# VectorE adds exponential tiles before the softmax row sum in six more units of a fused attention and MLP kernel

## The chip, the cores and the metric

The kernel runs on one core of a Trainium2 chip. The metric is the device time of one execution in microseconds (us), the median of several runs. Before the change it is 419.66 us, median of 3 runs (419.33 to 421.46). A core has a matrix engine (TensorE, "PE" in the profile, with its weight loads as "PEld"), VectorE ("DVE"), ScalarE ("ACT"), GpSimd ("POOL"), and DMA queues, most of which are issued by SyncE ("SP"). [...]engines wait for each other with semaphores.

## The reference

Attention with RMS-normalised queries and keys, for 8 batches of 12 heads, sequence 448, head size 64, followed by a two-layer MLP with a leaky ReLU. Everything in and out is float32.

```python
q_n, k_n = rmsnorm(q, g_q), rmsnorm(k, g_k)          # over the head size, 64
scores = (q_n @ k_n^T) / 8
attn = exp(scores - max(scores))
attn = attn / (sum(attn) + 1e-9)                     # the row sum
x = attn @ v                                         # -> (8*448, 12*64)
h = x @ w_in                                         # 768 -> 2048
out = maximum(0.01 * h, h) @ w_out                   # 2048 -> 768
```

## The kernel before

The heads are taken four at a time: a "unit" `u` is one group of four heads of one batch, so there are 24 units (`NU = 24`, three to a batch). The 448 keys of a unit are cut into seven steps `t` (`NS = 7`). For each step TensorE computes scores into one of two PSUM slots, and ScalarE takes the exponential into `et[:, t]`, a tile of 128 partitions by 2 by 448 in fp16.

A unit has four stages `d`: scores and exponentials of step 0, then 1 and 2, then 3 and 4, then 5 and 6. Between them TensorE is filled with items of the MLP from a queue, for an earlier batch.

```python
STEPS = ((0,), (1, 2), (3, 4), (5, 6))
def fill(u, d, jobs):
    ...                                   # how many items of the queue this stage takes
    while queue and debt[0] >= queue[0][0] * 0.5:
        c, fn = queue.pop(0)
        fn()                              # an MLP item: matmuls on TensorE
        debt[0] -= c
        if jobs:
            jobs.pop(0)()                 # one job behind each item
    flush()                               # work that the last item put off
    for job in jobs:
        job()                             # and the rest of the jobs
```

The row sum is a matmul of ones with the exponential tiles, accumulated in PSUM over the tiles. It happens one unit later, in stage 0 of unit `u + 1`. In most units it is `zcol`: for each tile four matmuls with a 128x32 block of ones and 224 columns, each into its own 32 PSUM partitions. In the first few units and the last it is `zsum_slot`: for each tile four matmuls with a 64x64 block of ones and 448 columns.

```python
def zsum_slot(u):
    ...
    ets = z_tiles(u)
    for i, e in enumerate(ets):
        for r in range(2):
            for a in range(2):
                nc.tensor.matmul(s["zt"][r][64 * a:64 * a + 64, 0:S], ones16[64 * r:64 * r + 64],
                                 e[64 * r:64 * r + 64, a], start=(i == 0), stop=(i == len(ets) - 1))

ADDED = {u: 4 for u in (10, 11, 13, 16, 17, 19)}
ADDED[NU - 1] = 5

def add_e(u):                             # VectorE sums the first ADDED[u] tiles into one
    s = st[u]
    s["ea"] = zpool.tile([P, 2, S], FP16, tag="ea", name="ea")
    for t in range(1, ADDED[u]):
        nc.vector.tensor_tensor(s["ea"], s["et"][:, 0] if t == 1 else s["ea"], s["et"][:, t], op=ALU.add)

def z_tiles(u):                           # what TensorE has left to sum
    s = st[u]
    ets = [s["et"][:, t] for t in range(NS)]
    return ets[ADDED[u]:] + [s["ea"]] if "ea" in s else ets

def zcol(u):
    ...
    ets = z_tiles(u)
    for i, e in enumerate(ets):
        for y in range(2):
            for a in range(2):
                c = 32 * (2 * y + a)
                nc.tensor.matmul(s["zc"][c:c + 32, 0:HS], onesr, e[:, a, HS * y:HS * y + HS],
                                 start=(i == 0), stop=(i == len(ets) - 1))
```

The main loop, cut to the parts that matter here. `shift_max` (VectorE) takes a bound on the scores from step 0 and spreads it on a diagonal `dg`; `shift_mm` (TensorE, then VectorE) turns that into the bias `eb` of the exponentials. Between the two, TensorE does the previous unit's product with v (`pv_slot`, `pv`) and its row sum.

```python
for u in range(3, NU):
    for d in range(4):
        if d > 0 or u > 3:
            qk(u, STEPS[d])                       # scores
            if d == 0:
                shift_max(u)
                ...
                if narrow(u - 1):                 # 4 <= u - 1 < 23
                    pv_slot(u - 1)
                    zcol(u - 1)
                    shift_mm(u)
                    pv_out(u - 1)                 # ScalarE frees the slot of pv
                else:
                    zsum_slot(u - 1)
                    pv(u - 1)
                    shift_mm(u)
                    zinv(u - 1)                   # ScalarE: 1 / row sum
            ex(u)                                 # exponentials
            if d == 0 and narrow(u - 1):
                zcol_ln(u - 1)
        if d == 2 and u in ADDED and u < NU - 1:
            add_e(u)
            xmul_sb(u - 1)                        # VectorE: pv times 1 / row sum
        jobs = []
        ...
        if d == 0:
            ...
            if u < 6:
                prep_sqp(u + 3)                   # GpSimd: squares for the norm
        if d == 1 and narrow(u - 1) and not 5 <= u < 8 and u not in ADDED:
            xmul_pool(u - 1)                      # the same product on GpSimd
        ...
        if d == 1 and 5 <= u < NU - 1:
            job(prep_g, u + 1)
        if u + 2 < NU:
            if d == 1:
                for ti in range(2):
                    job(prep_ssq, u + 2, ALL, (ti,))      # VectorE: sums of squares
            if d == 2:
                job(prep_rinv, u + 2)                     # ScalarE
                for ti in range(2):
                    job(prep_norm, u + 2, ALL, (ti,))     # VectorE
        ...
        if d == 1 and 4 <= u < 8:
            job(weight_sum, u - 4, 0)                     # VectorE
        ...
        fill(u, d, jobs)
```

The second MLP layer is done with fewer block products in some places, for which VectorE forms sums and differences of blocks of its operand (`sa`, by `s1` to `s4`). In units 8, 14 and 20 an MLP item puts off the first two of them (`s1`, `s2`) to the next `flush()`.

Of the kernel before, what the change touches and what calls it, by code (L numbers as in the profile page):

```python
# [18 lines left out]
def kernel(  # L19
# [18 lines left out]
    NU = B * NQ  # L38
# [91 lines left out]
    ALL = (0, NS)  # L130
# [7 lines left out]
    def buf(u, name):  # L138
        if name not in st[u]:
            shape, dtype, bufs = SHAPES[name]  # L140
            st[u][name] = prep_p.tile(shape, dtype, tag=name[:2] if bufs == 3 and name != "qkT" else name, bufs=bufs, name=name)
        return st[u][name]
# [14 lines left out]
    def prep_ssq(u, c=ALL, tis=BOTH):  # L157
        for ti in tis:
            nc.vector.tensor_reduce(buf(u, "ssq")[:, ti, :, c[0]:c[1]], buf(u, f"sq{ti}")[:, :, c[0]:c[1]],  # L159
                                    axis=AXL.X, op=ALU.add)  # L160
# [41 lines left out]
    def qk(u, steps):  # L202
        st[u]["sT"] = []
        for t in steps:
            sT = slot()
            score(u, t, (sT[:, 0], sT[:, 1]))
            st[u]["sT"].append((t, sT))
# [17 lines left out]
    def shift_max(u):  # L225
        s = st[u]
        sT = s["sT"][0][1]
        if isinstance(sT, list):
            pm2 = small.tile([P, 2], FP32, tag="pm2", name="pm2")
            for a in range(2):  # L230
                nc.vector.tensor_reduce(pm2[:, a:a + 1], sT[a][:, 0:S], axis=AXL.X, op=ALU.max)
            s["spare"] = sT[0]
            nc.vector.tensor_reduce(s["spare"][:, 511:512], pm2, axis=AXL.X, op=ALU.max)
        else:
            s["spare"] = sT[:, 0]
            nc.vector.tensor_reduce(s["spare"][:, 511:512], sT[:, :, 0:S], axis=AXL.XY, op=ALU.max)  # L236
        s["dg"] = small.tile([P, P], FP16, tag="dg", name="dg")
        nc.vector.tensor_tensor(s["dg"], ident16, s["spare"][:, 511:512].broadcast_to([P, P]), op=ALU.mult)
# [4 lines left out]
    def shift_mm(u):  # L243
        s = st[u]
        if u > 0 and "pslot" in st[u - 1]:
            pb = st[u - 1]["pslot"][:, :, S:S + 64]
            for x in range(2):
                nc.tensor.matmul(pb[:, x], onesp, s["dg"][:, 64 * x:64 * x + 64], start=True, stop=True)
            nc.vector.tensor_reduce(s["spare"][:, 510:511], pb, axis=AXL.XY, op=ALU.max)  # L249
        else:  # L250
            if "pb" not in s:
                shift_bank(u)
            pb = s["pb"]
            nc.tensor.matmul(pb[:, 0:P], onesp, s["dg"], start=True, stop=True)
            nc.vector.tensor_reduce(s["spare"][:, 510:511], pb[:, 0:P], axis=AXL.X, op=ALU.max)
        s["eb"] = small.tile([P, 1], FP32, tag="eb", name="eb")
        nc.vector.tensor_scalar(s["eb"], s["spare"][:, 510:511], -1.0, DELTA, op0=ALU.mult, op1=ALU.add)

    def gate(u):
        nc.gpsimd.tensor_copy(gate_t, buf(u, "n16")[:, 1, NS - 1, 1, D - 1:D])  # L260
# [21 lines left out]

    HS = S // 2
    ADDED = {u: 4 for u in (10, 11, 13, 16, 17, 19)}
    ADDED[NU - 1] = 5

    def add_e(u):
        s = st[u]
# [3 lines that stand above are left out]
# [6 lines left out]
    def zcol(u):  # L298
        s = st[u]
        s["zc"] = aux([P, 512], FP32, "zc")  # L300
# [8 lines that stand above are left out]
    def pv_slot(u):  # L309
        s = st[u]  # L310
        s["pslot"] = slot()
        s["pv"] = [s["pslot"][:, r] for r in range(2)]
        pv(u)
# [21 lines left out]
    def xmul_sb(u):  # L335
        xmul_pool(u, nc.vector)

    def xmul_pool(u, eng=nc.gpsimd):
        s = st[u]
        b, g = divmod(u, NQ)  # L340
        if b not in xts:
            xts[b] = xpool.tile([P, NQ, 2, S], FP16, tag="xt", name="xt")
        eng.tensor_tensor(xts[b][:, g], s["x32"], s["rz"], op=ALU.mult)  # L343
# [375 lines left out]
    def narrow(u):  # L719
        return 4 <= u < NU - 1  # L720
# [46 lines left out]
    with tc.manual_schedule():  # L767
# [182 lines left out]
# [3 lines that stand above are left out]
                    qk(u, STEPS[d])  # L953
                    if d == 0:
                        shift_max(u)
                        if u == 6:
                            xmul_sb(u - 2)
                        if narrow(u - 1):
# [3 lines that stand above are left out]
                            pv_out(u - 1)  # L962
# [4 lines that stand above are left out]
                            zinv(u - 1)  # L967
                    ex(u)
                    if d == 0 and narrow(u - 1):
                        zcol_ln(u - 1)  # L970
                if d == 2 and u in ADDED and u < NU - 1:
                    add_e(u)
                    xmul_sb(u - 1)
                jobs = []

                def job(fn, *args):
                    jobs.append(lambda: fn(*args))

                if d == 0:
                    if u == 3:  # L980
                        prep_norm(4)
                        gate(4)
                    elif narrow(u - 1):
                        if u < NU - 1:
                            job(zcol_inv, u - 1)
                    else:
                        xmul(u - 1)
                    if u + 4 < NU:
                        job(load, u + 4)
                    if u + 3 < NU:  # L990
                        load_v(u + 3)
                    if u < 6:
                        prep_sqp(u + 3)
                if d == 1 and narrow(u - 1) and not 5 <= u < 8 and u not in ADDED:
                    xmul_pool(u - 1)
                if u == NU - 1:
                    if d == 1:
                        job(zcol_inv, u - 1)
                if fed(u, d) and u > 3:
                    push(u // NQ - 1)  # L1000
                if (u, d) in ((3, 1), (4, 0)):
                    for ti in range(2):
                        prep_tr(u + 1, ti, VV)
                if d == 1 and 5 <= u < NU - 1:
                    job(prep_g, u + 1)
                if u + 2 < NU:
                    if d == 1:
                        for ti in range(2):
                            job(prep_ssq, u + 2, ALL, (ti,))
                    if d == 2:  # L1010
                        job(prep_rinv, u + 2)
                        for ti in range(2):
                            job(prep_norm, u + 2, ALL, (ti,))
                        if u > 3:
                            job(prep_trd, u + 2)
                if d == 1 and 4 <= u < 8:
                    job(weight_sum, u - 4, 0)
                if d == 0 and 5 <= u < 9:
                    job(weight_sum, u - 5, 1)
                if d == 2 and 6 <= u < 8:  # L1020
                    job(xmul_sb, u - 1)
                if u == NU - 2 and d == 0:
                    for n, tile_ in ((1, (raws, "rq", 3)), (2, (raws, "rk", 3)), (3, None), (4, (prep_p, "sq", 3))):
                        job(win_sum, n, 1, tile_)
                    for n in (3, 1, 2, 4):
                        job(x_sum, LATE, n)
                if u == NU - 1 and d == 3:
                    job(add_e, u)
                    job(xmul_sb, u - 1)
                if d == 3 and 6 <= u < NU - 3:  # L1030
                    for ti in range(2):
                        job(prep_sq, u + 3, ALL, (ti,))
                fill(u, d, jobs)
# [39 lines left out]
```

## Time and profile before

| | |
|---|---|
| Median time (lowest to highest of 3) | 419.66 us (419.33 to 421.46) |
| Span of the profiled execution | 418.4 us |
| TensorE busy | 402.0 us, 96% of the span |
| VectorE busy | 290.5 us, 69% |
| ScalarE busy | 303.6 us, 73% |
| GpSimd busy | 68.6 us, 16% |
| Mean TensorE clock granted | 0.99 of full speed |

The profile is of one execution. It has the busy time of each engine, the idle time of an engine before each group of instructions together with what ended it, the chain of work that ended last (followed back from the last instruction, at each step to what released it), and a timeline. In a timeline line stand the start and the length in us, then engine, line of the program, operation, and `output<-inputs` with shapes and the count; a bracket gives the idle time ahead of it and what ended it. "PE L306" are the row sums by `zcol`, "PE L280" those by `zsum_slot`, "DVE L291" the adds of `add_e`, "PE L248" and "PE L254" the matmuls of `shift_mm`, and "DVE L236" and "DVE L238" the two operations of `shift_max`.

### The profile page before, as it was taken

How to read it: one execution, taken by the hardware profiler on the slowest of the kernel's cores; microseconds unless marked ns; L12 is line 12 of the kernel's file. 1: busy time of each engine (PE TensorE's matmuls, PEld its weight loads, DVE VectorE, ACT ScalarE, POOL GpSimd, SP SyncE). 2: the span in 40 equal slices, each digit the busy share in tenths (PEclk: the TensorE clock that was granted, in tenths of full speed). 3: DMA queues.
4: the chain of work that ended last, by engine and by line, in shares of the span. 5: the costliest groups of instructions: out<-in, count | busy, mean ns of one | idle time of the engine just before them, and what ended most of it. 6: DMA issues, size and time to landing. Idle time of an engine off the chain costs nothing.

```text
span 418.4 us, 9417 instructions
## 1 busy us (share of the span) xinstructions
PE 402.0 (96%) x3871; PEld 220.6 (53%) x3871; DVE 290.5 (69%) x469; ACT 303.6 (73%) x474; POOL 68.6 (16%) x70
## 2 busy tenths in 40 slices
PE   7877999999999999999999999999999999999995
PEld 6544444555455444455445554455445557558863
DVE  5788675787658757767648757768548787557762
ACT  5998877868987679867986679967986657653600
POOL 1868422300020100020011100011001101000000
PEclk9699999999999999999999999999999999999999
DMA  6999998889664786677565787568552460032023
GB/s 202 268 254 251 240 250 137 194 161 209 166 154 68 209 193 148 169 162 175 153 144 107 205 171 173 148 130 196 171 111 46 119 152 14 2 83 78 0 56 96
DMA packets 71950, 62.41 MB, mean 149 GB/s; under 512 B 36324, under 2 KB 67044, under 8 KB 71908
## 3 DMA queue, kind: packets, MB, share of 16 engines
q1 hardware_dynamic: 61312, 49.62, 46.4%
q0 software_dynamic: 10272, 11.80, 17.8%
q8 instruction: 30, 0.49, 0.5%
q10 hardware_dynamic: 324, 0.39, 0.3%
q14 instruction: 12, 0.10, 0.1%
HBM read 45.61 MB, written 11.01 MB: 135 GB/s over the span
## 4 chain that ended last, share of the span: by engine, by line
PE 80%; ACT 8%; DVE 8%; issue 2%; DMA 1%; SPq 0%; DVEq 0%; ACTq 0%
PE hps L385 27%; PE sT L199 8%; PE sT L363 5%; PE ma L467 5%; PE md L467 5%; ACT et L218 4%; PE bank L587 4%; PE mc L467 4%; PE bank L467 4%; PE op L426 4%; PE mb L467 3%; PE zc L306 3%; DVE n L171 2%; PE sT L467 2%; PE bank L426 1%
## 5 line engine op out<-in xcount | busy, mean ns | idle before, releaser
L218 ACT ACTIVATE et<-sT,eb 128x896 f16<-128x896 f32 x166 | 159.3, 1009 | 18.8 <-PE sT L199 17.0
L385 PE MATMUL hps<-xt,win 128*128 128x448 f16 x600 | 120.8, 353 | 0.2 <-DVE xt L372 0.2
L385 PEld LDWEIGHTS <-win 128*128 128x128 f16 x612 | 56.8, 98 | 58.2 <-issue 9.7
L379 ACT ACTIVATE gt<-hps 128x448 f16<-128x448 f32 x100 | 53.9, 555 | 6.3 <-PE hps L385 5.4
L199 PE MATMUL sT<-qkT 64*64 64x448 f16 x664 | 53.2, 368 | 3.0 <-ACT et L218 1.9
L159 DVE TENSOR_REDUCE ssq<-sq 128x14 f32<-128x896 f32 (+2 forms) x49 | 50.3, 1058 | 0.7 <-ACT sq L148 0.7
L467 PEld LDWEIGHTS <-sa 128*128 128x128 f16 x352 | 32.8, 98 | 26.3 <-issue 6.1
L128 POOL DMA_DIRECT2D vt<-in_v_dram x24 | 17.9, 746 | 172.1 <-PE sT L363 164.7
L318 ACT COPY x<-sT 128x896 f32<-128x896 f32 x19 | 17.2, 905 | 35.4 <-DVE sT L249 35.4
L171 DVE TENSOR_TENSOR n<-rq,rinv 128x896 f16<-128x896 f32 (+2 forms) x25 | 27.6, 1107 | 13.6 <-ACT rinv L165 10.5
L467 PEld LDWEIGHTS <-gt 128*128 128x128 f16 x264 | 25.2, 98 | 19.7 <-issue 3.2
L199 PEld LDWEIGHTS <-qkT 64*64 64x64 f16 x672 | 15.2, 105 | 36.8 <-issue 33.2
L343 POOL TENSOR_TENSOR xt<-x,rz 128x896 f16<-128x896 f32 x9 | 19.0, 2111 | 81.8 <-DMA rz<-zs 81.8
L363 PE MATMUL sT<-et,vt 64*64 64x448 f16 x532 | 28.5, 349 | 0.3
L426 PE MATMUL op<-wout,gt 128*128 128x384 f16 x160 | 28.4, 326 | 0.0
L236 DVE TENSOR_REDUCE sT<-sT 128x1 f32<-128x896 f32 x22 | 24.1, 1094 | 4.7 <-PE sT L199 4.7
L363 PEld LDWEIGHTS <-vt 64*64 64x64 f16 x672 | 20.7, 107 | 11.3 <-issue 1.7
L171 DVE TENSOR_TENSOR n<-rk,rinv 128x896 f16<-128x896 f32 (+2 forms) x26 | 26.1, 1011 | 0.0
L426 PEld LDWEIGHTS <-gt 128*128 128x128 f16 x192 | 17.6, 98 | 14.3 <-issue 3.0
L467 PE MATMUL ma<-wout,gt 128*128 128x384 f16 x128 | 23.5, 326 | 0.0
L448 DVE TENSOR_TENSOR sa<-gt 128x512 f16<-128x512 f16 (+1 forms) x15 | 8.2, 545 | 16.9 <-ACT gt L379 12.2
L291 DVE TENSOR_TENSOR ea<-ea,et 128x896 f16<-128x896 f16 x15 | 9.4, 625 | 13.6 <-ACT et L218 13.3
(142 smaller groups left out, 541.5 us busy)
## 6 DMA issues: line engine op xcount, KB each, us to landing
rq<-in_q_dram SPq DMA_DIRECT2D x24, 448.0 KB, 3.7
rk<-in_k_dram SPq DMA_DIRECT2D x24, 448.0 KB, 5.3
out_dram<-ost SPq DMA_DIRECT2D x52, 192.0 KB, 3.1
rz<-zs SPq DMA_DIRECT2D x76, 112.0 KB, 2.3
vt<-in_v_dram POOLq DMA_DIRECT2D x24, 224.0 KB, 5.2
win<-in_moe_w_in_dram POOLq DMA_DIRECT2D x8, 384.0 KB, 13.4
wout<-in_moe_w_out_dram POOLq DMA_DIRECT2D x2, 1536.0 KB, 27.9
out_dram<-ost SPq DMA_DIRECT2D x4, 96.0 KB, 2.1
```

The source lines that it names most:

```text
L128: nc.gpsimd.dma_start(vts[u % NV].rearrange("p a t d -> p a (t d)"), rows(v, u))
L159: nc.vector.tensor_reduce(buf(u, "ssq")[:, ti, :, c[0]:c[1]], buf(u, f"sq{ti}")[:, :, c[0]:c[1]], axis=AXL.X, op=ALU.add)
L171: nc.vector.tensor_tensor(buf(u, "n16")[:, ti, c[0]:c[1]].rearrange("p s a d -> p a s d"), src[:, :, c[0]:c[1]], buf(u, "rinv")[:, ti, :, ...
L199: nc.tensor.matmul(banks[a][64 * r:64 * r + 64, 0:S].rearrange("p (t x) -> p t x", t=NS), kT(u, r, a, t), qT(u, r, a), start=True, stop=True)
L218: nc.scalar.activation(s["et"][:, t], sT[:, :, 0:S], AF.Exp, bias=s["eb"], scale=1.0)
L236: nc.vector.tensor_reduce(s["spare"][:, 511:512], sT[:, :, 0:S], axis=AXL.XY, op=ALU.max)
L343: eng.tensor_tensor(xts[b][:, g], s["x32"], s["rz"], op=ALU.mult)
L363: nc.tensor.matmul(s["pv"][r][64 * a:64 * a + 64, 0:S], vts[u % NV][64 * r:64 * r + 64, a, t], s["et"][64 * r:64 * r + 64, t, a], start=(t ...
L379: nc.scalar.activation(dst, src, AF.Prelu, bias=0.0, scale=1.0, alpha=0.01)
L385: nc.tensor.matmul(hps[:, 0:S], win16[:, kt // 2, kt % 2, ts(ft, P)], xt[:, kt // 2, kt % 2], start=(kt == 0), stop=(kt == KT - 1))
L426: nc.tensor.matmul(op2[:, 0:HC], gt[:, ft, ds(col(t), P)], wout16[:, ft, ds(HC * half, HC)], start=(ft == 0), stop=(ft == FT - 1))
L467: nc.tensor.matmul(bank[:, 0:HC], a[:, f], b[:, f], start=(first and f == 0), stop=(f == HF - 1), skip_group_check=not first)
```

## The change

VectorE sums exponential tiles in six more units, so that TensorE has fewer tiles left in the row sum. In units 3 and 4 it sums the first five tiles, at stage 2, ahead of the jobs of that stage. In units 8, 14 and 20 it sums the first three, at stage 1: there the two sums of squares and the adds become one job, which comes ahead of the put-off operand sums `s1` and `s2`. In unit 22 it sums the first three, as the third job of stage 1 (an empty job keeps the place). The conditions around `xmul_sb` and `xmul_pool` are kept such that the product with the inverse row sum stays where it was in all these units.

```diff
     ADDED = {u: 4 for u in (10, 11, 13, 16, 17, 19)}
-    ADDED[NU - 1] = 5
+    ADDED.update({3: 5, 4: 5, NU - 1: 5})
+    ADDED.update({u: 3 for u in (8, 14, 20, 22)})
@@
-                if d == 2 and u in ADDED and u < NU - 1:
+                if d == 2 and ADDED.get(u, 0) > 3 and u < NU - 1:
                     add_e(u)
-                    xmul_sb(u - 1)
+                    if u > 4:
+                        xmul_sb(u - 1)
@@
-                if d == 1 and narrow(u - 1) and not 5 <= u < 8 and u not in ADDED:
+                if d == 1 and narrow(u - 1) and not 5 <= u < 8 and ADDED.get(u, 0) < 4:
                     xmul_pool(u - 1)
@@
                     if d == 1:
-                        for ti in range(2):
-                            job(prep_ssq, u + 2, ALL, (ti,))
+                        if ADDED.get(u) == 3:
+                            job(lambda u: (prep_ssq(u + 2), add_e(u)), u)
+                        else:
+                            for ti in range(2):
+                                job(prep_ssq, u + 2, ALL, (ti,))
@@
                 if d == 2 and 6 <= u < 8:
                     job(xmul_sb, u - 1)
+                if d == 1 and u == NU - 2:
+                    jobs.append(lambda: None)
+                    job(add_e, u)
```

## The prediction, made before the changed kernel ran

> **What bounds the kernel now.** I read the shares of busy time first, then the chain that ended last, then the waits, then the timeline around the places that the change touches. The first two lines below are from the page of the kernel before: busy times, and the chain by engine.
>
> ```profile
> PE 402.0 (96%) x3871; PEld 220.6 (53%) x3871; DVE 290.5 (69%) x469; ACT 303.6 (73%) x474; POOL 68.6 (16%) x70
> ...
> PE 80%; ACT 8%; DVE 8%; issue 2%; DMA 1%; SPq 0%; DVEq 0%; ACTq 0%
> ```
>
> TensorE is busy for 96% and holds 80% of the chain. All the waits of TensorE for another engine add up to about 11 us, and most of them lie before 45 us. So a microsecond of matmuls taken out between 55 and 360 us is a microsecond off the end, provided TensorE does not start to wait for what replaces it. The saving is read from the row sums. The chain in order of time (start, length, what) shows one of each form, with what stands behind it:
>
> ```profile
> 55.89 1.32 PE sT L280 x28
> 57.21 1.32 PE pv L363 x28
> 58.53 0.18 PE pb L254
> ...
> 70.70 1.32 PE sT L363 x28
> 72.02 0.78 PE zc L306 x28
> 72.81 0.17 PE sT L248 x2
> ```
>
> Unit 3's row sum (L280) costs 1.32 us for 7 tiles, or 0.189 per tile. Unit 4's (L306) costs 0.78 for 7 tiles. The matmuls of one tile run side by side in the array: 28 of them, 259 ns each, take 0.78 us. A unit that already has four tiles added gives the marginal cost. Unit 16, in the timeline:
>
> ```profile
> 257.53 0.47 PE L306 MATMUL zc<-et,onesr 128*32 128x224 f16 x12
> 257.54 0.29 DVE L238 TENSOR_TENSOR dg<-ident,sT 128x128 f16<-128x128 f16 x1
> 257.83 0.27 PE L306 MATMUL zc<-ea,onesr 128*32 128x224 f16 x4
> ...
> 258.03 0.23 PE L248 MATMUL sT<-dg,onesp 128*128 128x64 f16 x2
> ```
>
> From 257.53 to the next matmul at 258.03 are 0.50 us for 4 tiles, against 0.79 for 7 in the units without adds (193.30 to 194.09): 0.097 us per tile and a fixed 0.11.
>
> [...]the 22 adds it has took 616 to 627 ns. [...]A `weight_sum` (L442) of 0.95 us took 1.66 where it began at 63.37, while GpSimd's square ran from 62.54 to 64.22: it ended 0.8 us after GpSimd. That bears on unit 3, below.
>
> **The change part by part.** Adding n tiles on VectorE costs n - 1 adds and takes n - 1 tiles from TensorE.
>
> Added on VectorE: 4 adds in each of units 3 and 4, 2 in each of 8, 14, 20, 22, together 16 x 0.625 = 10.0 us. Taken from TensorE: 4 x 0.189 = 0.75 us (unit 3), 4 x 0.097 = 0.39 (unit 4), 4 x 2 x 0.097 = 0.78 (the rest). That is 64 matmuls and 1.92 us at the most. The 10 us count only where they hold something up, so I go through the gaps.
>
> *Unit 3, stage 2.* The timeline around it:
>
> ```profile
> 48.90 2.07 DVE L159 TENSOR_REDUCE ssq<-sq 128x14 f32<-128x896 f32 x2
> 50.05 1.68 POOL L152 TENSOR_TENSOR sq<-rk 128x896 f32<-128x896 f32 x1 [0.71 <-DVE ssq L159]
> 50.87 1.90 ACT L218 ACTIVATE et<-sT,eb 128x896 f16<-128x896 f32 x2
> 53.75 1.09 DVE L171 TENSOR_TENSOR n<-rq,rinv 128x896 f16<-128x896 f32 x1 [2.78 <-issue]
> ```
>
> VectorE is idle for 2.78 us here, and four adds need 2.5. But the first add meets GpSimd's square, [...]so I let it end at about 52.25; the second at 52.9, the third at 53.5 and the fourth at 54.15 (tile 4 is ready at 52.77). The two norms then end near 56.25, and `shift_max` of unit 4, now at 56.01, starts 0.2 to 0.3 us late: `dg` at 57.7 instead of 57.43. With only three tiles in the row sum, TensorE reaches `shift_mm` at 58.47 - 0.75 = 57.72. So the saving here is 0.75, or 0.6 if `dg` comes last. I count 0.65. What follows (1 / row sum on ScalarE, the product on VectorE, the first MLP item that waits for it at 59.88) hangs on these matmuls and moves up with them.
>
> *Unit 4, stage 2.* VectorE is idle from 65.03 to 68.50, waiting for ScalarE's `rinv`. Tiles 3 and 4 are ready at 66.7 and 67.6, so the last add ends near 68.25, ahead of the norm. Nothing is delayed. The row sum of three tiles is 0.40 us from 71.95, to 72.35; `dg` is done at 72.24, and `shift_mm` can follow an end of `dg` after 0.05 us (177.94 to 177.99 in unit 12). So it starts at 72.35 instead of 72.74, and 0.39 is gained.
>
> *Units 8, 14, 20, stage 1.* The timeline of unit 14:
>
> ```profile
> 213.20 1.08 DVE L159 TENSOR_REDUCE ssq<-sq 128x14 f32<-128x896 f32 x1
> 214.81 1.92 ACT L218 ACTIVATE et<-sT,eb 128x896 f16<-128x896 f32 x2
> 217.83 0.43 DVE L448 TENSOR_TENSOR sa<-gt 128x512 f16<-128x512 f16 x1 [3.54 <-ACT gt L379]
> 218.29 0.43 DVE L451 TENSOR_TENSOR sa<-sa,gt 128x512 f16<-128x512 f16 x1
> 218.47 2.19 POOL L343 TENSOR_TENSOR xt<-x,rz 128x896 f16<-128x896 f32 x1 [7.17 <-DMA rz<-zs]
> 218.63 1.08 DVE L159 TENSOR_REDUCE ssq<-sq 128x14 f32<-128x896 f32 x1
> ```
>
> The gap of 3.54 us before `s1` takes the second sum of squares (to 215.3), and the adds end near 216.5 and 217.4, as tiles 1 and 2 come at 215.8 and 216.7. `s1` waits for ScalarE until 217.83 anyway. The 1.08 us that the second reduction took behind `s2` come free; I give nothing for that[...]. Unit 20 has the same gap (4.86 us), unit 8 one of 3.81. The saving is 0.19 each at `shift_mm`: `dg` was done 0.43 us before it in unit 15 (226.86 against 227.29), and in units 9 and 21 the same. Sum 0.58.
>
> *Unit 22.* VectorE waits 1.51 us before 346.89. The adds would end near 346.0 and 346.65 (tile 2 at 345.8), just before the copy needs the engine. In unit 23 `dg` ends at 357.02 and `shift_mm` starts at 357.31, so 0.19 fits.
>
> Sum: 0.65 + 0.39 + 0.58 + 0.19 = 1.8 us. On 419.66 this makes 417.9.
>
> **The rivals.** *VectorE's delay takes the place of the matmuls.* Between `shift_max` and `shift_mm` the row sum is also cover for VectorE: in unit 12, behind a row sum of four tiles, `shift_mm` already waits for `dg`. If the adds of unit 3 or 4 ran later than I think, these two savings (1.1 us) would go and the time would be 419. Against it: both gaps are nearly as long as the adds, and the rest of the units keep five tiles.[...]
>
> *The gain is taken up later.* In unit 9 one matmul (L467 at 144.65) waits 0.55 us for VectorE, which was blocked behind GpSimd's product (a norm of 1.08 us took 2.33). If that product is tied to its DMA and not to TensorE, up to 0.55 us of what units 3, 4 and 8 gained stays there, and the time is 418.4. If the shift parts the two, the wait vanishes and it is 417.4. Elsewhere the chain goes through ScalarE and VectorE only in pieces that begin at a TensorE instruction, so they move along.
>
> *The reordering itself helps.* Sums of squares done 1 us earlier let `rinv` start earlier. ScalarE waited only 0.15 us for them in unit 14, so this is worth at most 0.2 us in three units: 417.3.
>
> *More work makes VectorE the bound.* With 300.5 of 418 us it is still at 72%; against it.
>
> **Range and chances.** The matmuls cap the saving at 1.9 us, or 2.5 with a lost wait. The three runs lie within 0.3 us of each other but for one at 421.46, so I allow 0.4 us for the medians. The absorbing rivals reach 419.2. Range 416.9 to 419.2. Two per cent would be 8.4 us, which no step here comes near in either direction.
>
> **What would show it right or wrong.** In the changed profile: 64 matmuls fewer (about 3807), 16 DVE instructions more (485), DVE about 10 us and PE about 2 us apart from before. L291 should have 38 adds near 625 ns, except the first of unit 3, which should take over 1 us. From the start of L306 to L248 there should be 0.40 us in unit 5 and 0.60 in 9, 15, 21, 23, with no idle line "PE <- DVE dg" over 0.1 us. From the start of L280 to L254 in unit 4 there should be 2.0 us instead of 2.75. A longer span, a norm of unit 5 that ends after 56.5, or new waits for DVE on TensorE would show the first rival.

## The result, and the profile after

The changed kernel takes 418.12 us, median of 6 runs (417.61 to 419.21), against 419.80 for the kernel before (6 runs, 419.33 to 421.46). The ratio is 0.9958, with a 95% interval of 0.9938 to 0.9978: 0.4% faster, inside the predicted range and 0.2 us from the predicted 417.9. A second series gave 418.11 against 419.90 (0.9956, interval 0.9943 to 0.9970).

Two lines of the page of the changed kernel, busy times and the chain by engine:

```profile
PE 398.9 (96%) x3807; PEld 219.2 (53%) x3807; DVE 301.6 (72%) x485; ACT 303.6 (73%) x474; POOL 68.6 (16%) x70
PE 80%; DVE 8%; ACT 8%; issue 2%; DVEq 0%; ACTq 0%
```

64 matmuls are gone and 16 VectorE instructions have come, which add 11 us of VectorE time. TensorE's busy time fell by 3.1 us, more than the 2 us predicted; 2.0 of these lie between the starts of `shift_mm` in units 3 and 23 (311.4 to 309.4 us), where the matmuls were taken out, and the rest before and behind that. TensorE still holds 80% of the chain. By these totals the trade went through as drawn.

Where the time went is best read from one instruction that every unit has, the matmul of `shift_mm` (L254 up to unit 4, L248 from unit 5). Its start in the two traces, with the change from one row to the next as the step:

| start of `shift_mm` in unit | before | after | difference | step |
|---|---|---|---|---|
| 3 | 42.82 | 42.48 | -0.34 | (start of the program) |
| 4 | 58.47 | 57.44 | -1.03 | -0.69 |
| 5 | 72.74 | 71.27 | -1.47 | -0.44 |
| 9 | 131.64 | 129.98 | -1.66 | -0.19 |
| 10 | 148.47 | 146.10 | -2.37 | -0.71 |
| 15 | 227.29 | 224.73 | -2.56 | -0.19 |
| 21 | 322.51 | 320.31 | -2.20 | +0.36 |
| 23 | 357.31 | 354.90 | -2.41 | -0.19 |
| end of span | 418.4 | 416.0 | -2.4 | 0.0 |

In units left out the difference moves by 0.02 us at most. The first row is the prologue, whose end lies between 0.7 us earlier and 1.5 us later than before in the traces below; no part of the change is in it. From there on the steps add up to 2.07 us, while the medians differ by 1.7 to 1.8; the other 0.3 us are not accounted for. Five steps are those of the prediction. Two are not: 0.71 us gained in unit 9, where the change does nothing, and 0.36 lost in unit 20, where 0.19 should have been gained.

Unit 3's adds in the timeline of the changed kernel, and what follows:

```profile
49.70 1.68 POOL L152 TENSOR_TENSOR sq<-rk 128x896 f32<-128x896 f32 x1 [0.71 <-DVE ssq L159]
50.53 1.33 DVE L292 TENSOR_TENSOR ea<-et 128x896 f16<-128x896 f16 x1
51.97 2.08 DVE L292 TENSOR_TENSOR ea<-ea,et 128x896 f16<-128x896 f16 x3
53.97 1.08 DVE L171 TENSOR_TENSOR n<-rq,rinv 128x896 f16<-128x896 f32 x1
...
57.10 0.29 DVE L238 TENSOR_TENSOR dg<-ident,sT 128x128 f16<-128x128 f16 x1
57.44 0.23 PE L254 MATMUL pb<-dg,onesp 128*128 128x128 f16 x1
```

The first add began while GpSimd's square ran, took 1.33 us instead of 0.62, and ended 0.48 us behind the square. All four are done at 54.05, the norm follows without a gap, and `dg` ends 0.05 us before the matmul that reads it: here VectorE comes last, by a hair. In unit 5 the row sum is down to three tiles, and in unit 14 the adds lie in the gap ahead of `s1` (L449):

```profile
70.87 0.38 PE L307 MATMUL zc<-et,onesr 128*32 128x224 f16 x8
71.07 0.27 PE L307 MATMUL zc<-ea,onesr 128*32 128x224 f16 x4
71.27 0.23 PE L248 MATMUL sT<-dg,onesp 128*128 128x64 f16 x2
...
213.51 0.62 DVE L292 TENSOR_TENSOR ea<-et 128x896 f16<-128x896 f16 x1 [2.07 <-ACT et L218]
214.41 0.63 DVE L292 TENSOR_TENSOR ea<-ea,et 128x896 f16<-128x896 f16 x1 [0.27 <-ACT et L218]
215.46 0.43 DVE L449 TENSOR_TENSOR sa<-gt 128x512 f16<-128x512 f16 x1 [0.42 <-ACT gt L380]
```

And this is the step that went the wrong way, around the start of unit 21:

```profile
312.57 2.08 POOL L344 TENSOR_TENSOR xt<-x,rz 128x896 f16<-128x896 f32 x1 [8.61 <-ACT uu L164]
312.63 2.30 DVE L458 TENSOR_TENSOR sa<-gt,sa 128x512 f16<-128x512 f16 x1
...
319.97 0.29 DVE L238 TENSOR_TENSOR dg<-ident,sT 128x128 f16<-128x128 f16 x1
320.31 0.22 PE L248 MATMUL sT<-dg,onesp 128*128 128x64 f16 x2 [0.49 <-DVE dg L238]
```

GpSimd's product (L344) came late, an operand sum of 0.41 us (L458) was caught behind it for 2.30, VectorE never made that up, and nearly eight microseconds later TensorE waited 0.49 us for `dg`.

### The profile page after: what moved, and what is told of

Its sections match the earlier page's. It is cut to its first block, busy times and chain, and to the rows that moved or that the text cites. A ratio compares the mean times of both kernels' runs of the same rounds, so it can differ in the third digit from the quotient of the medians.

```text
span 416.0 us, 9315 instructions
## 1 busy us (share of the span) xinstructions
PE 398.9 (96%) x3807; PEld 219.2 (53%) x3807; DVE 301.6 (72%) x485; ACT 303.6 (73%) x474; POOL 68.6 (16%) x70
## 4 chain that ended last, share of the span: by engine, by line
PE 80%; DVE 8%; ACT 8%; issue 2%; DVEq 0%; ACTq 0%
PE hps L386 27%; PE sT L199 8%; PE sT L364 5%; PE ma L468 5%; PE md L468 5%; ACT et L218 5%; PE mc L468 5%; PE bank L588 4%; PE bank L468 4%; PE op L427 4%; PE mb L468 2%; PE zc L307 2%; DVE n L171 2%; PE warm L766 2%; PE sT L468 2%
## 5 line engine op out<-in xcount | busy, mean ns | idle before, releaser
L171 DVE TENSOR_TENSOR n<-rq,rinv 128x896 f16<-128x896 f32 (+2 forms) x25 | 26.2, 1050 | 9.5 <-ACT rinv L165 9.5
L344 POOL TENSOR_TENSOR xt<-x,rz 128x896 f16<-128x896 f32 x9 | 18.9, 2102 | 79.5 <-DMA rz<-zs 63.6
L292 DVE TENSOR_TENSOR ea<-ea,et 128x896 f16<-128x896 f16 x25 | 15.6, 625 | 15.6 <-ACT et L218 14.7
L292 DVE TENSOR_TENSOR ea<-et 128x896 f16<-128x896 f16 x13 | 8.8, 675 | 11.6 <-ACT et L218 11.6
```

The source lines that it names most:

```text
L171: nc.vector.tensor_tensor(buf(u, "n16")[:, ti, c[0]:c[1]].rearrange("p s a d -> p a s d"), src[:, :, c[0]:c[1]], buf(u, "rinv")[:, ti, :, ...
```

## The experiments

Three theories stood at the start. *The trade*: each step is the matmuls taken out, the adds are free, and the order of jobs is neutral. *The order*: moving the second sum of squares ahead of `s1` is what gains or loses. *Chance*: the steps in units 9 and 20 only show where one DMA landed in that execution. Later a fourth was needed.

**Units 3 and 4 alone.** The adds of the other four units are left out, and with them their order of jobs and the empty job of unit 22.

```diff
     ADDED.update({3: 5, 4: 5, NU - 1: 5})
-    ADDED.update({u: 3 for u in (8, 14, 20, 22)})
```

> The adds in units 3 and 4 alone; the other four units are as before. Theory (TensorE pays for the row sums and VectorE's adds are free): 1.1 us below the kernel before; the matmul behind the bound on the scores (L254, L248) starts 0.7 us earlier in unit 4, another 0.4 in unit 5, and no unit after that gains or loses more, but for a wait of about 0.55 us for VectorE that GpSimd's product can put anywhere. Rival (the order of jobs in units 8, 14, 20 gives the gain): under 0.6 us. First add of unit 3 about 1.3 us[...].

Measured: 418.37 us against 420.14, ratio 0.9958 (0.9942 to 0.9974). Steps of -0.68 and -0.44 in units 4 and 5 as expected. Unit 9 gained 0.71 again, and unit 12 lost 0.42. The medians differ by 1.8 us where 1.1 was expected; the steps of the trace add up to 1.4.

**Units 8, 14, 20 and 22 alone.**

```diff
-    ADDED.update({3: 5, 4: 5, NU - 1: 5})
+    ADDED.update({NU - 1: 5})
     ADDED.update({u: 3 for u in (8, 14, 20, 22)})
```

> The adds in units 8, 14, 20, 22 alone, with their order of jobs; units 3 and 4 are as before. Theory: 0.76 us below the kernel before, in four steps of 0.19 us at the starts of units 9, 15, 21, 23. Rival[...]: unit 21 starts with a wait for dg of 0.5 us again, and the whole is 0 to 0.3 us. Rival (order helps): over 1 us.

Measured: 418.86 us, ratio 0.9978 (0.9966 to 0.9989). The four steps came as 0.19, 0.19, 0.20 and 0.19, that of unit 21 too, without a wait, though the order of jobs there is that of the change. A further 0.35 came in unit 9. By the medians the whole is 1.3 us, where the rival that the order helps had asked for over 1; the next run tests that rival by itself.

**The order alone**, with both new lines of `ADDED` left out.

```diff
-                        if ADDED.get(u) == 3:
-                            job(lambda u: (prep_ssq(u + 2), add_e(u)), u)
+                        if u in (8, 14, 20):
+                            job(lambda u: prep_ssq(u + 2), u)
```

> No new adds at all: only the second sum of squares goes ahead of the operand sums in units 8, 14 and 20. Theory: the same as the kernel before within 0.2 us. Rival (the order costs time[...]): 0.2 to 0.6 us slower, with a wait for dg in unit 21. Rival (order helps, as sums of squares come earlier): 0.2 to 0.6 us faster.

Measured: 419.98 us, ratio 0.9995 (0.9985 to 1.0006). Every step after the prologue is 0.01 or less, but for +0.12 in unit 9. The order alone is worth nothing.

**All adds, and all matmuls.** VectorE does the 16 adds, and TensorE sums all seven tiles all the same.

```diff
-        return ets[ADDED[u]:] + [s["ea"]] if "ea" in s else ets
+        return ets[ADDED[u]:] + [s["ea"]] if "ea" in s and u not in (3, 4, 8, 14, 20, 22) else ets
```

> All adds of the change are done and left unused in units 3, 4, 8, 14, 20, 22: TensorE sums all seven tiles there as before. So VectorE has its 10 us more and TensorE keeps its 64 matmuls. Theory: the same as before within 0.3 us, because every add lies in a gap. Rival (VectorE's work delays the path): 0.5 us or more slower.

Measured: 420.19 us, ratio 1.0005 (0.9994 to 1.0016). All 10 us of adds cost nothing that can be seen; no unit's start moved by over 0.01 us, but for -0.37 in unit 9.

**Fewer matmuls, and no adds.** The tiles that VectorE would have added are left out of the row sum, so the result lacks them.

```diff
     def z_tiles(u):
         s = st[u]
         ets = [s["et"][:, t] for t in range(NS)]
+        if u in NEW:                      # NEW = (3, 4, 8, 14, 20, 22)
+            return ets[ADDED[u] - 1:]
@@
     def add_e(u):
+        if u in NEW:
+            return
```

> The changed kernel with the new adds left out, and the tiles that they would have summed left out of the row sum too (its output has too small a row sum in units 3, 4, 8, 14, 20, 22). TensorE does the same 64 matmuls fewer, VectorE has no extra work. Theory (the matmuls are the whole gain, the adds are free): the same as the changed kernel within 0.3 us, thus about 1.7 us below the kernel before; unit 4's step is 0.75 instead of 0.69, because dg no longer comes late. Rival (the adds cost something that the savings hide): 0.5 us or more below the changed kernel.

Measured: 418.20 us against 419.90, ratio 0.9951 (0.9931 to 0.9970), with a span of 415.9 us against the changed kernel's 416.0. Unit 4's step is 0.76 and unit 5's 0.39, the others are the same, and so are the two odd ones: -0.71 in unit 9 and +0.37 in unit 20, with the same wait of 0.49. Its unit 20 and the start of unit 21, to be held against the last fence of the changed kernel:

```profile
312.76 2.07 POOL L349 TENSOR_TENSOR xt<-x,rz 128x896 f16<-128x896 f32 x1 [8.96 <-DMA rz<-zs]
312.80 2.97 DVE L171 TENSOR_TENSOR n<-rq,rinv 128x896 f16<-128x896 f32 x1
...
320.16 0.22 PE L248 MATMUL sT<-dg,onesp 128*128 128x64 f16 x2 [0.49 <-DVE dg L238]
```

Here the norm is the operation that is caught behind the product (2.97 us instead of 1.09). So the wait comes without the adds as well. This run and the one before it settle the trade: the gain is TensorE's, and the adds cost 0.07 us at the start of unit 4, of which unit 5 gives 0.05 back.

**The second sum of squares put back behind `s2`.**

```diff
-                            job(lambda u: (prep_ssq(u + 2), add_e(u)), u)
+                            job(lambda u: (prep_ssq(u + 2, ALL, (0,)), add_e(u)), u)
+                            job(prep_ssq, u + 2, ALL, (1,))
```

> The changed kernel with the second sum of squares of units 8, 14, 20 put back behind the operand sums, and only the adds ahead of them. [...]no wait for dg at the start of unit 21, whenever the product lands, and steps of 0.19 us in units 9, 15, 21, 23. Time: 0 to 0.3 us below the changed kernel. If the wait in unit 21 only came from a late DMA, the order makes no difference.

Measured: 418.47 us, ratio 0.9966 (0.9954 to 0.9978). A miss: the wait at the start of unit 21 is not gone but longer, 0.86 us, and the step +0.74. The product was as late as in the changed kernel (it began 5.85 us after its transfer was issued), and with the reduction behind `s2` VectorE had one operand sum fewer done by then: L455, through in 0.41 us ahead of the product in the changed kernel, was caught for 2.21. The time is 0.4 us above the changed kernel in the same series (418.11), where 0 to 0.3 below was expected.

**Unit 7 too**, on top of that: a gap of 5 us that the change leaves unused.

```diff
-    ADDED = {u: 4 for u in (10, 11, 13, 16, 17, 19)}
+    ADDED = {u: 4 for u in (7, 10, 11, 13, 16, 17, 19)}
@@
-                if d == 2 and 6 <= u < 8:
+                if d == 2 and u == 6:
                     job(xmul_sb, u - 1)
```

> As the run before it, and unit 7 too: four tiles summed in VectorE's gap of 5 us at stage 2, with the product by the inverse row sum drawn ahead of the norm. Unit 8 should start its second part 0.29 us earlier: the row sum takes 0.50 us instead of 0.79, and dg comes 0.3 us earlier, as the product no longer stands ahead of the last two operand sums. Time: 0.3 us below the run before it, about 2.0 to 2.3 us below the kernel before. If dg still comes late: no difference.

Measured: 416.85 us (6 runs, 416.74 to 417.44) against 419.90, ratio 0.9921 (0.9901 to 0.9942). Unit 8 starts its second part 0.30 us earlier, as expected. But 1.6 us were gained on the run before it, where 0.3 were expected, and 0.9 of them lie at the start of unit 21: its step is -0.19 and there is no wait, with the same code for unit 20 as in the run where it was 0.86. The remaining 0.4 show in the medians and not in the steps.

**The changed kernel again.**

> The changed kernel again, for a second trace and more times. The steps of 0.69 (unit 4), 0.44 (5) and 0.19 (9, 15, 23) come again. If the waits in unit 9 (before) and at the start of unit 21 (after) depend on when one DMA lands in that execution, they fall differently here: unit 21 has its step of 0.19 and no wait for dg. If the order of jobs makes the wait, it is there again at 0.5 us.

Measured: 418.11 us, ratio 0.9956. All steps came again, and the odd ones too: -0.71 in unit 9, +0.36 in unit 20 with a wait of 0.49 us. So the theory of chance falls as well: whatever makes the product late there is part of the program. Nor is it a shift in time, as the second trace is 1.1 us behind the first from the prologue on.

**What makes the product late.** In all ten traces by then, GpSimd's product began either about 4.4 us after its transfer of 1 / row sum was issued (4.3 to 4.8), or 5 to 6.4. The transfer is four DMAs, 512 packets of 896 bytes in all. In nine late ones (those of the table below, but for its last row), all packets but eight were through at about the usual time, 3.8 to 4.1 us after the issue, and the eight followed one by one, some 0.1 us apart. Eight is a sixteenth of the last DMA's 128, and the page speaks of 16 DMA engines, so my guess was that one of them was behind. One queue of the profile moves packets of another size. Its line in the kernel before, and then in the changed one:

```profile
q8 instruction: 30, 0.49, 0.5%
```

```profile
q8 instruction: 29, 0.48, 0.5%
```

0.49 MB in 30 packets is 16 KB each, and the page calls the queue "instruction". TensorE has 2 x 3871 = 7742 matmuls and weight loads before and 7614 after, thus 258 and 263 to a packet; with the 128 fewer there is one packet fewer. From the start of one packet to the start of the next, TensorE began 253 instructions on average in the trace before and 254 in the one after, VectorE 20 and 21. So I take this queue to fetch TensorE's program. The packet of a fetch took 0.9 to 1.7 us. Set against the first issue of the transfer, from the packet records:

| unit, kernel | fetch begins after the issue | product begins after the issue |
|---|---|---|
| 9, before | 3.30 | 6.27 |
| 9, order alone | 3.31 | 6.39 |
| 9, all adds and all matmuls | 3.35 | 5.90 |
| 9, units 8, 14, 20, 22 alone | 3.45 | 5.92 |
| 9, after (both traces) | none | 4.66, 4.70 |
| 20, before | none | 4.36 |
| 20, after (both traces) | 3.17, 3.10 | 5.80, 5.77 |
| 20, second sum of squares behind | 3.17 | 5.85 |
| 20, fewer matmuls and no adds | 3.82 | 6.16 |
| 20, unit 7 too | 3.84 | 4.35 |
| 12, units 3 and 4 alone | 3.12 | 6.06 |
| 18, before | 0.47 | 5.31 |

In every late case with a fetch at 3.1 us or later, the first of the eight packets ended within 0.1 us of the end of the fetch. In unit 20 of the changed kernel the fetch ended at 4.30 and the eight at 4.40 to 5.06; without a fetch in the way (unit 20 before) all 512 were through at 3.85. The records don't name a packet's engine; that the two met on one engine is my inference from this. A fetch at 3.8 us comes as the last packets go, which may be why 3.82 was late and 3.84 was not.

That gave a fourth theory: the change moves the waits by taking instructions from TensorE's list, so that its fetches fall elsewhere. The three last runs change nothing but the number of idle matmuls that keep TensorE busy in the prologue.

**The changed kernel with 16 idle matmuls fewer.**

```diff
-        warm(42, wbank)
+        warm(26, wbank)
```

> The changed kernel with 26 instead of 42 idle matmuls[...] (they end before TensorE waits for VectorE at 7.2 us). 32 instructions fewer in TensorE's list, nothing else. Theory (a fetch of 16 KB of instructions [...]holds back the 1 / row sum transfer that it meets): the fetch in unit 20, 3.2 us after the issue of that transfer in the changed kernel, comes about 1 us later, after the transfer; GpSimd's product starts 4.4 us after the issue instead of 5.8, no wait for dg at the start of unit 21, its step is -0.19 instead of +0.36. Time 0.4 to 0.6 us below the changed kernel. Rival (the order of jobs in unit 20 makes the wait): it stays at 0.5 us.

Measured: 417.22 us against 419.95, ratio 0.9951 (0.9937 to 0.9965). The timeline of this run, to be held against the last fence of the changed kernel:

```profile
311.05 2.21 POOL L344 TENSOR_TENSOR xt<-x,rz 128x896 f16<-128x896 f32 x1 [7.15 <-DMA rz<-zs]
...
313.46 0.41 DVE L458 TENSOR_TENSOR sa<-gt,sa 128x512 f16<-128x512 f16 x1
...
319.17 0.29 DVE L238 TENSOR_TENSOR dg<-ident,sT 128x128 f16<-128x128 f16 x1
...
319.70 0.23 PE L248 MATMUL sT<-dg,onesp 128*128 128x64 f16 x2
```

The fetch comes 4.25 us after the issue, the product begins at 4.34, the operand sum takes its 0.41 us, and the matmul no longer waits. The step is -0.19. The order of jobs is that of the change, so it is not by itself what made the wait. The medians of the two series put this run 0.9 us below the changed kernel, the ratios 0.2 to 0.3; the step accounts for 0.55, as expected. Unit 14's step is -0.13 here instead of -0.19.

**The kernel before with 16 idle matmuls fewer.** The same edit.

> The kernel before with the same 16 idle matmuls fewer. Theory: the fetch that comes 3.3 us after the issue in unit 9 moves behind the transfer; GpSimd's product starts 4.5 to 4.7 us after the issue instead of 6.3, it no longer meets the norm, TensorE's wait of 0.55 us there goes, and unit 10 starts 0.7 us earlier without any part of the change. Time 0.5 to 0.7 us below the kernel before, if no other transfer is met. Rival (the earlier start through units 3 and 4 took the wait away): it stays.

Measured: 419.63 us, ratio 0.9988 (0.9981 to 0.9995): 0.5 us by the ratio and 0.3 by the medians, the small end of what was expected or below it, but the step in unit 9 is -0.72 and stands alone. The fetch now comes 5.20 us after the issue instead of 3.30, and the product begins at 4.56 instead of 6.27. Unit 9 in the kernel before, and then in this run:

```profile
141.11 2.07 POOL L343 TENSOR_TENSOR xt<-x,rz 128x896 f16<-128x896 f32 x1 [9.11 <-DMA rz<-zs]
141.80 2.33 DVE L171 TENSOR_TENSOR n<-rq,rinv 128x896 f16<-128x896 f32 x1 [0.31 <-ACT rinv L165]
...
144.65 1.46 PE L467 MATMUL md<-tw,gt 128*128 128x384 f16 x8 [0.55 <-DVE ost L474]
```

```profile
138.68 2.08 POOL L343 TENSOR_TENSOR xt<-x,rz 128x896 f16<-128x896 f32 x1 [7.40 <-DMA rz<-zs]
...
141.08 1.09 DVE L171 TENSOR_TENSOR n<-rq,rinv 128x896 f16<-128x896 f32 x1 [0.32 <-ACT rinv L165]
...
143.21 1.46 PE L467 MATMUL md<-tw,gt 128*128 128x384 f16 x8
```

The product ends at 140.76, ahead of the norm, instead of running into it. Nothing of the change is in this kernel: the 0.71 us that the changed kernel gained in unit 9 need no more than a shorter list of TensorE instructions ahead of that point (32 fewer here, 64 fewer through units 3 and 4); an earlier start isn't needed.

**Unit 7 too, with 11 idle matmuls more.**

```diff
-        warm(42, wbank)
+        warm(53, wbank)
```

> The version with unit 7 too, with 53 instead of 42 idle matmuls at the start (they fit into the 0.7 us that TensorE waits there). 22 instructions more ahead of everything. Theory: the fetch in unit 20, 3.8 us after the issue, comes back to about 3.2 us, the product starts at 5.8 again, and unit 21 starts with a wait for dg of 0.5 to 0.9 us. Time 0.5 to 0.9 us above the version with 42. Rival: no change.

Measured: 418.14 us, ratio 0.9962 (0.9946 to 0.9978), 1.3 us above the version with 42 by the medians of two series, and 0.93 us by the step in unit 20 (+0.74 instead of -0.19). The fetch is back at 3.14 us, the product at 5.85, and unit 21 starts with a wait of 0.87 us. One part of the expectation failed: the idle matmuls did not fit into TensorE's wait. They took 3.96 us in this trace, against 2.52 for the 42 in the other one, and TensorE's next matmul started at 8.99 us without a wait, instead of at 8.00 after a wait of 0.40. The step in unit 20 is free of that, the whole time need not be.

Over all 13 traces there are 117 such transfers. In 15 the product began over 4.9 us after the issue, and in 14 of these a fetch had begun within the first 3.7 us; only one transfer with a fetch in that time was not late. Between 3.75 and 3.91 it went either way (one late in nine). The 15 are of two kinds. In ten the fetch began at 3.1 to 3.8 us, and the product began 3.7 to 4.4 us after the last of the four issues instead of about 2.5. In the other five the fetch began 0.2 to 0.6 us after the first issue, and it is SyncE's issues that were late: the last came 2.5 to 2.9 us after the first instead of 1.9, and the product about 2.5 after that. Why an issue is held up is open.

## Why the prediction was right, and where it was wrong

*What bounds the kernel*: right. The fewer-matmuls run and the all-matmuls run show that TensorE's row sums carry the gain and that VectorE's 10 us (11 measured) are off the path. The adds took 0.61 to 0.63 us each in the trace (0.625 predicted), but for the one of 1.33 beside GpSimd's square.

*Unit 3, 0.65 us*: right in size and in its course. Measured 0.67 to 0.69; 0.76 without the adds. The first add was given about 1.3 us and took 1.33, and `dg` did come last: it was put at 57.7, and ended at 57.39 in a trace that is 0.34 us ahead of the one before at that point.

*Unit 4, 0.39 us*: measured 0.44 to 0.45 in every run that has the adds, 0.39 without them. So the 0.05 over the sum come with the adds: part of the 0.07 that the late `dg` cost at the start of unit 4 seems to be made up within that unit.

*Units 8, 14, 20 and 22, 0.19 each*: right in 8, 14 and 22, and in 20 wherever the product is on time.

*The second rival*, that the wait in unit 9 may stay or vanish: it vanished, as the prediction had it for "if the shift parts the two". The cause was named wrongly: not that TensorE's start shifts against a DMA, but that no fetch falls among the DMA's packets any more (one 3.30 us after the issue before, none after).

*"No idle line PE <- DVE dg over 0.1 us"*: wrong. Unit 21 has one of 0.49. The step that failed is "`dg` was done 0.43 us before it in unit 15 ... and in units 9 and 21 the same", which carried the slack of the trace before over to unit 21: the gap in unit 20 was there, but I took the product's start from the trace before as fixed. By the prediction's own signs this new wait would have spoken for the first rival, VectorE's delay; the run without adds has the same wait, so that sign misleads here. A late product in unit 9 that vanished and one in unit 20 that came nearly cancel, so it is in part luck that the sum of 1.8 us was met. The steps of the change without the prologue are -2.07 us in its trace, of which 0.71 are unit 9's and +0.55 unit 20's shortfall; the rest is -1.9, the cap in the prediction.

*The third rival*, that the order helps by up to 0.2 us: it didn't (0.9995). With the product late, the order of the change makes the wait 0.49 us where the other one makes it 0.86 or 0.87, so it has some use, but only there.

## What to carry to other kernels

When TensorE is busy nearly throughout, a tile sum moved to VectorE is worth the matmuls' marginal time, provided the adds fit in a gap that ends with a wait for something else; the worth of a step could be read from the trace before to 0.05 us here (0.65, 0.39 and 0.19 predicted, 0.69, 0.44 and 0.19 measured). When a step appears in a stage that the edit doesn't touch, look at what else an edit changes, here the place of the instruction fetches: two small variants of the same program with a few harmless instructions more or fewer tell that apart in one go. A late transfer cost nothing in unit 18 of the kernel before: the product began 5.31 us after the issue there and at 4.37 in the changed kernel, a norm beside it took 1.29 us instead of 1.09, and the start of unit 19 has no step (0.00). It cost half a microsecond in unit 20 of the changed kernel, where GpSimd's product ran beside a VectorE operation with both inputs in SBUF and that took 2.30 us instead of 0.41. So give VectorE slack where such a product can land, or work of the kinds that took no longer beside it (the last section has them; no run here tries that).

## What the runs showed of the hardware that I had not expected

- Transfers of the kernel landed late where a fetch of what I take for TensorE's program fell among them. A fetch is a packet of 16 KB that took 0.9 to 1.7 us, one about every 13 us here (30 from 13.3 to 399.6 us in the kernel before). GpSimd's product, which waits for a transfer of 512 small packets, began up to 1.9 us later (6.39 us after the issue in unit 9 with the order alone, 4.53 with units 3 and 4 alone), and eight packets came behind the fetch.
- So the number of instructions ahead of a point changed the time after it: 16 idle matmuls fewer in the prologue, with their weight loads, moved the start of unit 10 by 0.72 us in one kernel and that of unit 21 by 0.55 in the other.
- VectorE operations with both inputs in SBUF that began during a GpSimd elementwise operation took longer in all 13 cases of the traces before and after, and ended 0.28 to 0.95 us behind it: an operand sum 2.30 us instead of 0.41, one of unit 14 in the kernel before 0.85 instead of 0.42, a norm 2.33 instead of 1.09, a weight sum 1.66 instead of 0.95, the add of unit 3 1.33 instead of 0.62. A sum of squares, with one input, took its 1.08 us there too (218.63 us in the kernel before), and products and sums with one of their two inputs in PSUM took no longer either: 0.61 us for `xt<-pv,rz` and 0.56 for `ost<-mc,ost`.
